# A new issue order for an attention and two-expert-layer kernel, from a planner with other prices, and a statistics buffer of eight turns

## The chip, the cores and the metric

The kernel runs on one core of a Trainium2 chip. The metric is device time in microseconds (us), lower is better; a value is the median of several runs. One further execution was recorded by the profiler; all rows below are from it. The engines are named as in the rows: PE (TensorE; PEld is its weight load), DVE (VectorE), ACT (ScalarE), POOL (GpSimd), and SP, which issues nearly all DMAs.

## The reference

```python
# q_l, k_l, v_l: (4, 8, 512, 64); q_g, k_g, v_g: (4, 8, 32, 64)
s_g = scale * q_g @ concat(k_g, k_l).T ;  out_g = softmax(s_g) @ concat(v_g, v_l)
s_l = concat(scale * q_l @ k_g.T, where(|i - j| <= 32, scale * q_l @ k_l.T, -1e9))
out_l = softmax(s_l) @ concat(v_g, v_l)
x = concat(out_g, out_l)                       # 2176 tokens x 512
h = x @ w_in ; solu = h * softmax(h)           # 512 -> 1024
x = layernorm(solu) * g_ln @ w_out             # 1024 -> 512
logits = x @ phi                               # 32 slots, 4 for each of 8 experts
slot_input = softmax(logits, axis=0).T @ x
slot_out[e] = relu(slot_input[e] @ w1[e]) @ w2[e]
out = softmax(logits, axis=1) @ slot_out       # 2176 x 512
```

## The kernel before

**Stages.** 16 local attention tiles (`local_tile`: 4 batches, 4 tiles of 128 queries) and 4 global ones (`global_tile`) give x. 17 dense tiles of 128 tokens (`dense_tile`) make h, its statistics, the normalised rows, the 32 logits, and add their part to the slot inputs as soon as x is there; attention, dense tiles and the loading of weights are interleaved over the first 230 us. `tail` runs the eight experts and the output product.

**What sets the order.** No order is written by hand. Every piece of work is an `op` with an engine, a price in ns and a number from the table `PRIORITY`. `Schedule.run` plays a time line with those prices: a free engine takes, among its ops whose inputs are ready in that time line, the one of lowest priority number. The result is one fixed sequence for each engine, and that sequence is what the program holds. On the chip each engine walks its own sequence and waits at a row whose inputs are late, whatever stands behind it. So a price, a cap or a priority acts only through the sequence; nothing of it is there at run time. The prices the change touches are:

- `LAT`: from the end of an op on one engine to the start of one on another; the entry `("DVE", "SP")` is that from a DVE copy to a DMA issue that reads it.
- `Fetch`: the planner holds that PE's instructions come in blocks of 256, and that a block can't be entered sooner than `TIME` ns after the one ahead of it was.
- `CAPS` and `KEEP`: how many buffers of a class may be alive at once, and how many are held back for a class. `STAY`: what PE adds to the priority of an op that changes its tiling.

**Lines the prediction speaks of.** L742: scores, one op is 32 products, which the profile counts as 64 matmuls. L755 (ACT): exp. L772: transposes of a tile of E, 4 to an op. L787, L862: attention times v. L899: x times `w_in`, half an op is 6 matmuls (wh, wl are high and low parts of the weights). L606, L607, L608 (DVE): three passes that make a weight, `W` or `wo`, out of the loaded words `wst`; L683 transposes `wo`. L983, L1049: logits and slot sums. L914 to L973 use the statistics `st`. L882: matmuls on a constant, into a bank that nothing reads (`warm`). In the tail L1177 and L1224 are the experts' products, L1258 the output product, L1264 and L1266 its copies by ACT and DVE, L1271 and L1273 the stores.

The last of the output, 192 columns wide, is stored in four DMAs of 384 KB and one small one:

```python
fs -> so -> sb                  # expert sums, once for 320 columns, once for 192
for j0 in range(0, 17, group):  # L1258, copies, then store() of one unit
    op("SP", ..., lambda store=store: store(nc.sync), obr, ())
```

Of the kernel before, what the change touches and what calls it, by code (L numbers as in the profile page):

```python
# [10 lines left out]
F32 = mybir.dt.float32  # L11
# [24 lines left out]
    ("SP", "SP"): 2600, ("PE", "SP"): 1270, ("ACT", "SP"): 1270, ("DVE", "SP"): 1270, ("Pool", "SP"): 1270,  # L36
# [68 lines left out]
class Fetch:  # L105
# [11 lines left out]
    def run(self, o, t, d):  # L117
        room = self.BLOCK - self.n % self.BLOCK
        if o.count >= room:
            self.entered = t + d * room / o.count  # L120
            self.TIME = 6400.0 if self.entered < 62000 else 5000.0
            self.n += o.count
            return True
        self.n += o.count
        return False


class Schedule:
# [8 lines left out]
    def buf(self, pool, tag, shape, dtype=F32, bufs=1):  # L137
        return Buf(self, pool, tag, shape, dtype, bufs, None)
# [228 lines left out]
def rank(names, name):  # L367
# [6 lines left out]
CAPS = dict(h=10, p1=67, E=20, W=52, eT=32, lT=8, ln=35, q=40, u=20, v=53, wst=20, xhl=72, xp=20)  # L374
KEEP = dict(p1=1, E=2, W=2, eT=2, eg=16, lT=1, ln=3, mkx=8, q=1, u=2, v=2, w=6, wo=5, wst=5, xhl=4, xp=1)
# [13 lines left out]
STAY = 1.13106627204  # L389
# [120 lines left out]
def kernel_body(ctx: ExitStack, tc: tile.TileContext, q, k, v, w_in, w_out, phi, gl, w1, w2, cst, out):  # L510
# [3 lines left out]
    buf, slot, op = sch.buf, sch.slot, sch.op  # L514
# [9 lines left out]
    mkx = slot("sb", "mkx", [128, 2, 512])  # L524
# [17 lines left out]
    wo = [Region(wob[f // 2], lambda a, f=f: a[:, f % 2, :]) for f in range(8)]  # L542
    egs = slot("sb", "eg", [128, 1024])
    eg = Region(egs, lambda a: a[:, 0:768])
# [341 lines left out]
    def dense_tile(j):  # L886
        X = xt[j]
        xhl = slot("sb", "xhl", [128, 2, 4, 128], F32R)
# [13 lines left out]
        st = buf("hw", "st", [128, 12], F32, 3)  # L902
# [532 lines left out]
```

## Time and profile before

| what | value |
|---|---|
| median of 3 runs | 295.19 us (294.35 to 296.47) |
| profiled execution | 295.09 us, of which 293.3 us are the span that the rows cover |
| PE busy | 265.0 us, 90% of the span, 4378 matmuls |
| DVE, ACT, POOL busy | 202.6 us, 196.1 us, 102.1 us |
| first matmul, end of the last one | 12.0 us, 286.1 us |
| PE clock | 1.00 of full speed in every stretch up to 285 us |
| DMA | 75.23 MB; mean 256 GB/s over the span |
| instruction packets of PE's queue (q8) | 34, 0.56 MB |
| kernel's share of the chain that ended last | PE 80%, DVE 6%, DMA 5%, ACT 4% |

Times in rows are from the span's start. A row of an instruction group has its start, its duration, engine, line, operation, the buffers written and read, and in brackets what its engine waited for just before. "issue" as a releaser means that the profile shows no instruction or transfer that the engine waited for. Matmuls overlap, so the duration of one is longer than the time it adds; in the chain of waits a piece has the time that it adds.

### The profile page before, as it was taken

The page shows a single profiled execution, that of the slowest core. Times are in us where ns is not written, and L with a number is a line of the kernel's source. Part 1 is how long each engine was busy: PE and PEld are TensorE (multiplying, and loading weights), DVE is VectorE, ACT ScalarE, POOL GpSimd, SP SyncE. Part 2 cuts the span into 40 slices and gives each one's busy share as a digit, 9 for nine tenths or more (in the row PEclk, how much of TensorE's full clock was granted, in tenths as well). Part 3 has the DMA queues.
Part 4 walks back from the last instruction along what each step waited for, and adds up shares of the span by engine and source line. Part 5 has one row for each costly group of instructions (what it writes and reads, how often), then busy time and mean ns, then how long its engine had stood idle before and what let it go on. Part 6 is the DMA issues. An engine that isn't in the chain of part 4 may idle for free.

```text
span 293.3 us, 10933 instructions
## 1 busy us (share of the span) xinstructions
PE 265.0 (90%) x4378; PEld 199.0 (68%) x4378; DVE 202.6 (69%) x752; ACT 196.1 (67%) x650; POOL 102.1 (35%) x171
## 2 busy tenths in 40 slices
PE   0259789999999999999999999989999999999990
PEld 0248577877877887787877878868778774354670
DVE  1889989999864799859797888379769840110450
ACT  3498998875897799997799876555567732020350
POOL 3787775922202516331321424134234333100000
PEclk9999999999999999999999999999999999999996
DMA  7999999916885002625892759986847997999476
GB/s 253 378 401 415 401 405 404 373 64 254 288 329 175 11 6 74 220 81 161 276 378 72 253 158 327 378 323 235 233 166 251 339 353 250 323 348 291 150 263 202
DMA packets 33532, 75.23 MB, mean 256 GB/s; under 512 B 2889, under 2 KB 15817, under 8 KB 33097
## 3 DMA queue, kind: packets, MB, share of 16 engines
q1 hardware_dynamic: 33348, 74.43, 72.0%
q8 instruction: 34, 0.56, 0.8%
q14 instruction: 18, 0.14, 0.1%
q10 hardware_dynamic: 132, 0.10, 0.1%
HBM read 67.83 MB, written 4.46 MB: 246 GB/s over the span
## 4 chain that ended last, share of the span: by engine, by line
PE 80%; DVE 6%; DMA 5%; ACT 4%; issue 2%; SPq 0%; DVEq 0%; ACTq 0%
PE h L899 30%; PE p L1224 5%; PE p L787 5%; PE p L742 5%; PE p L1177 5%; PE p L772 4%; PE p L962 4%; DMA q<-in_q 3%; PE p L983 3%; PE p L1049 3%; PE p L882 2%; PE p L862 2%; PE p L1258 2%; PE p L851 2%; DMA mkx<-in_cst 2%
## 5 line engine op out<-in xcount | busy, mean ns | idle before, releaser
L899 PE MATMUL h<-w,xhl 128*128 128x512 f32 x408 | 107.2, 405 | 0.9 <-issue 0.8
L899 PEld LDWEIGHTS h<-w,xhl 128*128 128x128 f32 x408 | 72.5, 188 | 17.7 <-issue 3.6
L755 ACT ACTIVATE E<-E,nmx 128x128 f32<-128x128 f32 x128 | 49.8, 394 | 1.9 <-DVE nmx L750 1.9
L742 PE MATMUL p<-k,q 64*32 64x128 f32 x1024 | 21.2, 291 | 16.8 <-DMA k<-in_k 12.0
L750 DVE CUSTOM_DVE_ANT_0 E<-p,mkx 128x128 f32<-128x128 f32 x128 | 28.9, 284 | 4.0 <-PE p L742 3.9
L742 PEld LDWEIGHTS p<-k,q 64*32 64x32 f32 x1024 | 15.9, 112 | 21.0 <-issue 15.8
L919 ACT ACTIVATE u<-h,st 128x512 f32<-128x512 f32 x34 | 23.1, 687 | 6.6 <-DVE st L915 6.6
L891 POOL TENSOR_TENSOR xhl<-xp,xhl 128x512 fp32r<-128x512 f32 x16 | 20.6, 1288 | 16.8 <-ACT xhl L890 16.6
L922 DVE SCALAR_TENSOR_TENSOR u<-h,u 128x512 f32<-128x512 f32 x34 | 22.9, 683 | 3.7 <-ACT u L919 3.5
L755 ACT ACTIVATION_READ_ACCUMULATOR E<-E,nmx 128x1 f32 x128 | 24.7, 193 | 0.0
L914 DVE TENSOR_REDUCE st<-h 128x1 f32<-128x512 f32 x34 | 22.5, 684 | 1.8 <-PE h L899 1.6
L772 PE MATMUL p<-cs,E 128*128 128x128 f32 x128 | 20.1, 288 | 1.2 <-ACT E L755 1.2
L774 ACT ACTIVATE eT<-p 128x512 f32<-128x512 f32 x32 | 18.4, 593 | 3.7 <-PE p L772 3.6
L968 ACT ACTIVATE u<-ln 128x1024 f32<-128x1024 f32 x17 | 18.1, 1062 | 3.4 <-DVE ln L941 3.4
L973 POOL TENSOR_TENSOR st<-st,eps 128x1 f32<-128x1 f32 x17 | 10.8, 635 | 25.9 <-DVE st L970 25.7
L787 PE MATMUL p<-v,eT 128*32 128x64 f32 x1024 | 18.8, 226 | 0.4 <-issue 0.2
L787 PEld LDWEIGHTS p<-v,eT 128*32 128x32 f32 x1024 | 16.6, 114 | 3.6 <-issue 1.2
L772 PEld LDWEIGHTS p<-cs,E 128*128 128x128 f32 x128 | 15.7, 149 | 4.3 <-ACT E L755 1.4
L967 ACT ACTIVATE lT<-p 128x512 f32<-128x512 f32 x25 | 14.3, 592 | 6.1 <-PE p L962 6.1
L926 POOL TENSOR_SCALAR st<-st 128x1 f32<-128x1 f32 x17 | 5.2, 307 | 34.2 <-ACT u L919 26.7
L794 DVE TENSOR_TENSOR eT<-p,r 128x256 f32<-128x256 f32 x32 | 12.6, 417 | 5.1 <-PE p L787 2.1
L617 POOL TENSOR_SCALAR W<-W 128x512 f32<-128x512 f32 x8 | 11.9, 1492 | 8.5 <-ACT W L616 8.5
(144 smaller groups left out, 550.6 us busy)
## 6 DMA issues: line engine op xcount, KB each, us to landing
unit<-in_w SPq DMA_DIRECT2D x47, 512.0 KB, 5.9
v<-in_v SPq DMA_DIRECT2D x28, 512.0 KB, 7.0
k<-in_k SPq DMA_DIRECT2D x3, 1536.0 KB, 6.4
k<-in_w SPq DMA_DIRECT2D x9, 512.0 KB, 5.1
wst<-in_w_in SPq DMA_DIRECT2D x8, 512.0 KB, 9.8
wst<-in_w_out SPq DMA_DIRECT2D x8, 512.0 KB, 9.1
q<-in_q SPq DMA_DIRECT2D x6, 512.0 KB, 5.6
out<-unit SPq DMA_DIRECT2D x8, 320.0 KB, 4.3
```

The lines of the kernel that those rows point to most:

```text
L742: nc.tensor.matmul(out=sp[hh][32 * c : 32 * c + 32, a2 + i, :], lhsT=Q[rows, 4 * (a2 + i) + c, :], rhs=K[rows, c, s : s + 128], start=True ...
L750: nc.vector.tensor_tensor_reduce(out=E[:, hh, a, :], in0=sp[hh][:, a, :], in1=MK(mask_kind(4 * t + a)), scale=-SCALE, scalar=3.0e38, op0=A ...
L755: nc.scalar.activation(out=E[:, hh, a, :], in_=E[:, hh, a, :], func=AF.Exp, bias=nmx[:, hh, a : a + 1], scale=-1.0, accum_out=sm[:, hh, a ...
L772: nc.tensor.transpose(out=tp[:, a, :], in_=E[:, hh, a, :], identity=I())
L774: op("ACT", 478, lambda hh=hh, tp=tp: nc.scalar.activation(out=eT[hh].ap, in_=tp.ap, func=AF.Copy), (tp,), (eT[hh],))
L787: nc.tensor.matmul(out=av[32 * c : 32 * c + 32, hh, a, :], lhsT=eT[hh][:, a, 32 * c : 32 * c + 32], rhs=V[:, (g - 1) % 2, 64 * h : 64 * h ...
L891: op("Pool", 1250, lambda: nc.gpsimd.tensor_tensor(out=xl.ap, in0=X.ap, in1=xh.ap.bitcast(F32), op=ALU.subtract), (X, xh), (xl,), port=True)
L899: nc.tensor.matmul(out=hp[n].ap, lhsT=lhs[:, kt, :], rhs=rhs[kt][n].ap, start=(kt == 0 and lhs is xh and rhs is whi), stop=(kt == 3 and lh ...
L914: op("DVE", 602, lambda n=n: nc.vector.tensor_reduce(out=part(7 + n), in_=hp[n].ap, axis=AX.X, op=ALU.max, negate=True), (hp[n],), (col[7 ...
L919: op("ACT", 664, lambda n=n: nc.scalar.activation(out=u[:, n, :], in_=hp[n].ap, func=AF.Exp, bias=nm(), scale=1.0, accum_out=part(7 + n)), ...
L922: op("DVE", 613, lambda n=n: nc.vector.scalar_tensor_tensor(out=u[:, n, :], in0=hp[n].ap, scalar=1.0, in1=u[:, n, :], op0=ALU.mult, op1=AL ...
L968: op("ACT", 1040, lambda: nc.scalar.activation(out=flat(), in_=ln.ap, func=AF.Square, accum_out=ssq()), (*cens, lT[0]) if last else (cen,) ...
```

## The change

The planner gets other prices and limits: 2000 ns instead of 1270 from ACT or DVE to an SP issue that reads their result; 8200 ns instead of 6400 for a block of instructions entered between 30 and 37 us of its time line; 60 ns more for an op of the output product; other caps, holds and tiling bias. The table `PRIORITY` is another one throughout. The ring of statistics buffers `st`, one of which a dense tile uses, has 8 turns instead of 3. With that, the sequences of all engines are made anew. No op is added or removed: both programs have the same count of every line on PE, and the same DMAs. One line is inserted above line 505, so lines behind it are one higher in the changed kernel (L742 is L743 there).

```diff
-    ("SP", "SP"): 2600, ("PE", "SP"): 1270, ("ACT", "SP"): 1270, ("DVE", "SP"): 1270, ("Pool", "SP"): 1270,
+    ("SP", "SP"): 2600, ("PE", "SP"): 1270, ("ACT", "SP"): 2000, ("DVE", "SP"): 2000, ("Pool", "SP"): 1270,
...
-            self.TIME = 6400.0 if self.entered < 62000 else 5000.0
+            self.TIME = 5000.0 if self.entered >= 62000 else 8200.0 if 30000 < self.entered < 37000 else 6400.0
...
-CAPS = dict(h=10, p1=67, E=20, W=52, eT=32, lT=8, ln=35, q=40, u=20, v=53, wst=20, xhl=72, xp=20)
-KEEP = dict(p1=1, E=2, W=2, eT=2, eg=16, lT=1, ln=3, mkx=8, q=1, u=2, v=2, w=6, wo=5, wst=5, xhl=4, xp=1)
+CAPS = dict(h=12, p1=63, E=23, W=58, eT=24, lT=9, ln=29, q=37, u=20, v=50, wst=18, xhl=73, xp=24)
+KEEP = dict(E=2, W=1, eT=2, eg=4, lT=1, ln=3, mkx=2, q=2, u=2, v=6, w=14, wo=13, wst=4, xhl=4, xp=1)
...
-STAY = 1.13106627204
+STAY = 1.25705078264
...
 PRIORITY = """
-    -183421268 -188124029 6107468 -191252955 -193517899 29194840 37980178 36241030 -25836497 -188321516 28516688 94766979 -40409399 32268522 76499126
...
-        st = buf("hw", "st", [128, 12], F32, 3)
+        st = buf("hw", "st", [128, 12], F32, 8)
...
-                    op("PE", max(0.417 * w + 20, 110) * 2 * m, cmm, (ct, sb), pos, tiled=2, count=4 * m)
+                    op("PE", max(0.417 * w + 20, 110) * 2 * m + 60, cmm, (ct, sb), pos, tiled=2, count=4 * m)
```

In the rows of a sequence below, names carry a running number of the buffer, which differs between the two programs.

**First place: PE behind the score op in which it halted at 35.8 us.** PE before, from the end of that score op (p_91 and p_92 are its banks) to the next one:

```order
L742 MATMUL p_92_560<-k_429,q_334 32x128
L899 MATMUL h_82_519<-w_527,xhl_390 128x512 x3
L899 MATMUL h_82_519<-w_336,xhl_390 128x512 x3
L899 MATMUL h_618<-w_161,xhl_536 128x512 x3
L899 MATMUL h_618<-w_147,xhl_536 128x512 x3
L772 MATMUL p_103_638<-cs_72,E_478 128x128 x4
L742 MATMUL p_106_650<-k_429,q_334 32x128
```

PE in the changed program, from the end of the score op at the same place (p_90 and p_91):

```order
L743 MATMUL p_91_558<-k_393,q_463 32x128
L900 MATMUL h_85_530<-w_515,xhl_391 128x512 x3
L900 MATMUL h_85_530<-w_335,xhl_391 128x512 x3
L900 MATMUL h_616<-w_454,xhl_539 128x512 x3
L900 MATMUL h_616<-w_147,xhl_539 128x512 x3
L900 MATMUL h_649<-w_161,xhl_539 128x512 x3
L900 MATMUL h_649<-w_103,xhl_539 128x512 x3
L684 MATMUL p_111_669<-cs_78,wo_603 128x128 x2
L743 MATMUL p_113_673<-k_393,q_463 32x128
```

What moved: a third half of a dense tile stands ahead, the transposes of E went behind, and the transposes of `wo_603` (before: `wo_605`, three halves of L899 later) came forward.

DVE in the changed program at that place, where `wo_603` is made (its sequence before has the same rows under other names, from E_561 to wo_605):

```order
L915 TENSOR_REDUCE st_627<-h_85_530 128x1
L751 ISA E_559,nmx_607<-p_90_557,mkx_81 128x128
L751 ISA nmx_607 128x1
L607 TENSOR_SCALAR p_102_637<-wo_603 128x512
L608 SCALAR_TENSOR_TENSOR p_102_637<-wst_474,p_102_637 128x512
L609 SCALAR_TENSOR_TENSOR wo_603<-wst_474,p_102_637 128x512
```

Nothing moved here: DVE still makes this weight behind the scores of the same tile and behind the first row maximum of h.

**Second place: PE around the 18th border of 256 instructions, near 130 us.** Before, from the dense tile that follows a score op:

```order
L899 MATMUL h_2378<-w_527,xhl_2030 128x512 x3
L899 MATMUL h_2378<-w_336,xhl_2030 128x512 x3
L1014 MATMUL p_366_2348<-cs_72,lps_2292 128x128
L1014 MATMUL p_371_2366<-cs_72,lps_2334 128x128
L851 MATMUL p_391_2472<-cs_72,eg_66 128x128 x3
L772 MATMUL p_394_2480<-cs_72,E_2034 128x128 x4
L983 MATMUL p_396_2489<-lT_2352,pb_1495 32x128 x8
L1049 MATMUL p_398_2501<-ln_2148,D_2478 32x256 x4
L1049 MATMUL p_399_2508<-ln_2104,D_2476 32x256 x4
```

The changed program, from the attention product of a global tile:

```order
L863 MATMUL p_350_2230<-v_968,eT_2420 32x64 x8
L984 MATMUL p_395_2496<-lT_2381,pb_1535 32x128 x8
L1050 MATMUL p_398_2508<-ln_2002,D_2489 32x256 x4
L788 MATMUL p_370_2362<-v_1408,eT_2159 32x64 x4
L788 MATMUL p_370_2362<-v_1391,eT_2159 32x64 x8
L788 MATMUL p_370_2362<-v_2122,eT_2159 32x64 x4
L1050 MATMUL p_400_2534<-ln_1379,D_2492 32x256 x4
L743 MATMUL p_402_2542<-k_2267,q_2261 32x128
L743 MATMUL p_403_2543<-k_2267,q_2261 32x128
```

What moved: no dense tile and no full transposes stand between these 256 instructions any more; they are 48 matmuls of L863, 16 of L984, 16 of L1050, 32 of L788 and the beginning of a score op.

**Third place: the end.** SP, the last stores before (unit_4826 is the second half of a pair whose first is unit_4821; unit_4843 comes from the output product after it):

```order
L1273 DMA out<-unit_4793 4x32x320
L1271 DMA out<-unit_4796 128x4x192
L1271 DMA out<-unit_4821 128x4x192
L1271 DMA out<-unit_4843 128x4x192
L1271 DMA out<-unit_4826 128x4x192
```

SP in the changed program (unit_4825 is the second half of that pair, unit_4848 comes after it):

```order
L1274 DMA out<-unit_4792 4x32x320
L1272 DMA out<-unit_4796 128x4x192
L1272 DMA out<-unit_4821 128x4x192
L1272 DMA out<-unit_4825 128x4x192
L1272 DMA out<-unit_4848 128x4x192
```

The last two stores changed places. PE at the last output product, before (between the banks p_823, p_824 and p_827, p_828 of the output product):

```order
L1258 MATMUL p_823_4811<-ct_4772,ct_4516 128x192
L1258 MATMUL p_824_4812<-ct_4772,ct_4516 128x192
L882 MATMUL p_688_4149<-cs_72 128x128
L1258 MATMUL p_827_4829<-ct_4772,ct_4516 128x192
L1258 MATMUL p_828_4830<-ct_4772,ct_4516 128x192
```

PE in the changed program at the same place:

```order
L1259 MATMUL p_823_4810<-ct_4771,ct_4513 128x192
L1259 MATMUL p_824_4811<-ct_4771,ct_4513 128x192
L883 MATMUL p_687_4147<-cs_78 128x128 x6
L1259 MATMUL p_827_4834<-ct_4771,ct_4513 128x192
L1259 MATMUL p_828_4835<-ct_4771,ct_4513 128x192
```

Five matmuls on a constant moved from behind the last output product to ahead of it.

## Rows read from the trace of the kernel before

**Rows 1.** Waits of PE: us in total, times, longest.
```profile
PE p L742 <- DMA k<-in_k: 12.0, 1, 12.0
...
PE p L742 <- issue: 2.2, 3, 1.7
PE p L683 <- DVE wo L608: 1.3, 1, 1.3
```

**Rows 2.** Busy time by stretch: start:end, length, five engines, clock, DMA share, GB/s.
```profile
36.00:244.00 208.00, 204.24 (x3401) 161.67 (x3400) 165.58 (x630) 159.96 (x543) 74.46 (x140) 1.00 0.67 236
```

**Rows 3.** Chain of waits, 35 to 41 us: start, us, what.
```profile
35.79 1.69 issue
37.47 0.45 PE p L742 x15
37.92 2.96 PE h L899 x12
```

**Rows 4.** DMA queues, 34 to 37 us: packets, MB, share of 16 engines.
```profile
q8 instruction: 1, 0.02, 2.1%
```

**Rows 5.** Stretches around two halts; the second count is that of weight loads.
```profile
0.00:171.55 171.55, 151.89 (x3006) 120.66 (x3010) 142.22 (x564) 142.97 (x496) 75.29 (x111) 1.00 0.68 246
0.00:174.10 174.10, 154.44 (x3136) 122.95 (x3136) 144.62 (x570) 144.59 (x499) 75.86 (x112) 1.00 0.67 243
...
0.00:186.34 186.34, 166.49 (x3258) 132.32 (x3262) 152.83 (x595) 152.34 (x522) 80.17 (x119) 1.00 0.69 248
...
0.00:190.85 190.85, 171.00 (x3388) 136.10 (x3389) 154.69 (x602) 153.92 (x526) 80.71 (x120) 1.00 0.70 251
```

**Rows 6.** As rows 2: ahead of these two halts, and near 130 us.
```profile
130.00:136.00 6.00, 6.00 (x182) 4.64 (x170) 5.78 (x31) 6.00 (x27) 1.36 (x4) 1.00 0.29 94
...
171.55:173.90 2.35, 2.35 (x136) 2.18 (x136) 2.19 (x7) 1.62 (x5) 0.57 (x1) 1.00 0.20 33
186.34:190.81 4.47, 4.47 (x145) 3.74 (x135) 1.82 (x7) 1.58 (x5) 0.50 (x1) 1.00 0.97 373
```

**Rows 7.** Timeline of PE, the first matmuls after these two halts.
```profile
174.37 0.42 PE L787 MATMUL p<-v,eT 128*32 128x64 f32 x14 [0.19 <-issue]
...
192.21 0.51 PE L899 MATMUL h<-w,xhl 128*128 128x512 f32 x1 [0.78 <-issue]
```

**Rows 8.** Chain of waits, 132 to 137 us: what four kinds of op add.
```profile
132.95 0.57 PE p L983 x16
133.53 0.92 PE p L1049 x16
134.45 0.80 PE p L862 x48
135.25 1.03 PE p L787 x64
```

**Rows 9.** Timeline of DVE, the end of the first `wo` weight after the halt.
```profile
42.05 0.69 DVE L608 SCALAR_TENSOR_TENSOR wo<-wst,p 128x512 int32<-128x512 int32 x1
```

**Rows 10.** Page, costliest groups: busy, mean ns, idle before it and its releaser.
```profile
L914 DVE TENSOR_REDUCE st<-h 128x1 f32<-128x512 f32 x34 | 22.5, 684 | 1.8 <-PE h L899 1.6
```

**Rows 11.** Timeline from 283 us: copies and warm matmuls, then SP's last two stores.
```profile
283.24 1.02 DVE L1266 COPY unit<-p 128x384 f32<-128x384 f32 x2 [0.43 <-PE p L1258]
...
284.58 0.56 DVE L1266 COPY unit<-p 128x384 f32<-128x384 f32 x1 [0.32 <-PE p L1258]
...
284.65 1.42 PE L882 MATMUL p<-cs 128*128 128x128 f32 x11
...
285.20 0.80 SPq L1271 DMA_DIRECT2D out<-unit  x1
...
286.05 1.49 SPq L1271 DMA_DIRECT2D out<-unit  x1
```

**Rows 12.** Stretch in which the last stores move; below it their time to landing.
```profile
285.00:291.00 6.00, 1.07 (x10) 0.83 (x8) 0.14 (x1) 0.24 (x2) 0.00 (x0) 0.74 0.92 283
...
DMA to landing us min/median/max: 6.1/6.2/6.3
```

204 rows, old and new, of the table PRIORITY are left out of this document.

## Prediction

> **What bounds the kernel now.** I read the waits of PE first, since PE is busy for 90% of the span. They are short [rows 1]: one wait of 12.0 us for the first keys, then nothing longer than 1.7 us. The busy time by stretch says how much is left: between 36 and 244 us PE works 204.24 of 208.0 us at full clock [rows 2]. DVE and ACT work 162 and 160 us there, so PE is the bound, and an order that lost no time at all would gain 208.0 − 204.24 = 3.8 us in that stretch, 1.3% of the whole. A new order can take away idle time of PE and nothing else, because both programs hold the same operations: the same count of each line on PE, and by the sequences 99 and 100 changes of PE's tiling.
>
> Before 36 us the sequences of all engines are the same up to a few swapped rows. The first scores still need the same loads, and the chain there goes through the same DVE rows. I take 0 for that stretch. From 219 us to the last output products the sequences again agree, and I take 0 there too.
>
> So three things are left: the halts of PE that are called "issue", new waits between 36 and 219 us, and the stores at the end.
>
> **The halts.** The waits put 2.2 us in three halts on L742 [rows 1]; the largest is 1.69 us at 35.79 us, inside a score op of which 15 matmuls are left [rows 3]. Its operands are there, since the products ahead of it read the same k and q. What is under way is an instruction packet of PE's queue [rows 4]. Two more halts are 0.19 and 0.78 us [rows 7]. Counting matmuls and weight loads between halts gives their rule: from 171.55 to 174.10 us it is 130 + 126 = 256, from 186.34 to 190.85 us 130 + 127 = 257 [rows 5]. PE goes on at 174.37 and 192.21 us [rows 7], that is 2.8 and 5.9 us after it crossed the border 256 instructions earlier; ahead of the first of these DMA moved 33 GB/s, ahead of the second 373 [rows 6]. I read it as a block of 256 instructions that comes some time after the one ahead of it was entered, later when DMA is busy. A halt is that time less the work that 256 instructions hold.
>
> The planner's 8200 ns is meant for the halt at 35.79 us. It lets the planner know of the wait; it doesn't make the packet come. In the changed program the border falls into the score op at the same place (first place in the sequences), and the operations of the block ahead of it are the same. I take a halt of the same size: **0**. The bounds are −1.7 (no halt) and +0.5.
>
> Elsewhere the work in a block changes. The densest new one is the 18th, near 130 us (second place in the sequences): 48 matmuls of L862, 16 of L983, 16 of L1049, half of 64 of L787 and about 15 of L742. That is 0.80 + 0.57 + 0.92 + 0.52 [rows 8] + 0.45 [rows 3] = 3.3 us. DMA moves 94 GB/s there [rows 6], so 2.8 us is the nearer price and there is no halt; by the dearer price, 5.9 us, it would be 2.6. Other blocks get longer or shorter by less than 1 us: the one before 88 us and the one before 191 us, which halt now, hold about 0.4 us more work each, and three that don't halt hold 0.2 to 0.7 less. I take **0** for all of these, with −1.5 (the halts of [rows 7] and half a us more go) to +1.7 (two thirds of the dear price in one block).
>
> The Trainium skill, page "Runtime: NRT & Kernel Launch", section "Instruction fetch mechanics", says that a sequencer fetches blocks of 256 instructions through a DMA queue of its own while the one ahead executes, and that crossing a border is mostly hidden. The count of 256 agrees with the two stretches of [rows 5]; that it is hidden does not, by the 1.69 us of [rows 3]. By that rule there would be no price for a border, and the sum below would be lower by 2.2 + 0.2 + 0.8 = 3.2 us [rows 1, 7].
>
> **A new wait at 42 us.** Behind the halt, PE before does twelve matmuls of L899 in 2.96 us, 0.247 each [rows 3]. In the changed sequence 18 matmuls of L899 stand there, from 37.92 us to 37.92 + 18 x 0.247 = 42.37, and behind them the transposes of a `wo` weight. DVE's rows ahead of that weight are the same as before, and its last pass ends at 42.05 + 0.69 = 42.74 us [rows 9]. The row maximum that DVE takes ahead of it reads the first six of these matmuls, as before, so DVE is not later. PE waits 0.37 us and the hand-over, together about **+0.6**. The bounds are 0 (halt longer by 0.5) and +1.3, what the same wait cost once before [rows 1]. Behind it in PE's sequence are the next scores; DVE still has work for 0.3 us and more, so nothing else runs dry.
>
> **The ring of eight.** L914, the first writer of `st`, waits for PE's h alone, 1.6 of its 1.8 us [rows 10], never for a buffer. More turns remove no wait and add no instruction: **0**, both ways.
>
> **The end.** The last DVE copies before end at 283.24 + 1.02 = 284.26 us, which makes the second store of the pair ready. SP doesn't issue it: the store ahead in its sequence waits for the copy that ends at 284.58 + 0.56 = 285.14, goes out at 285.20, and the ready one only at 286.05 [rows 11]. It lands 6.3 us later, at 292.3 [rows 12]. Swapped, the ready one goes out at about 284.3. The last one still needs the last output product, and in front of this stand five more warm-ups, 5 x (1.42/11) = 0.65 us at most [rows 11], about 0.5 since PE had a short idle there. It goes out at 285.14 + 0.5 = 285.7 instead of 286.05, 0.35 earlier. The DMA engines have 8% of 6 us = 0.5 us to spare between 285 and 291 us [rows 12], and the earlier store lets them use it and the time ahead of 285. So the gain is between 0.35 and 0.9; I take **−0.6**. The bounds are 0 (the warm-ups eat it all) and −1.7 (the ready store was issued 286.05 − 284.3 = 1.75 us late and all of it comes back).
>
> **The sum.** 295.09 (the profiled execution) + 0 + 0 + 0.6 + 0 − 0.6 = **295.1 us**. The profiled execution is 0.1 us under the median of the three runs, 295.19, so nothing has to be added for that.
>
> **Rivals.**
>
> *Halts go away.* The planner's price may make the sequence put other work where the halt was, or the fetch may be earlier for a reason that I don't see. The halt at 35.79 us and half of the others vanish, and the wait at 42 us grows into its bound, since PE is earlier by 1.7 us: 295.1 − 1.7 − 0.8 + 0.7 − (the rest of the tail) 0.4 = 292.9 us. For it speaks that all of PE's idle time between 36 and 244 us is 3.8 us [rows 2] and mostly of this kind; against it, that the same rows stand around the border. With the wait hidden too it is 292.2, the floor.
>
> *Dense blocks halt (the other side).* If the time to the next block is 5.9 us and not 2.8 in a stretch of light DMA, the 18th block halts for 2.6 us; the 20th, near 147 us, holds about 3.1 us of work and halts for 2.8 (before, it held little more and did not halt). Both: 295.1 + 5.4 = 300.5; one of them and some tenths in two others: 295.1 + 3.2 = 298.3 us, which is what I take for this rival. It decides when the packet lands more than about 1.5 us later than in the stretch at 171.55 us. Against it: DMA moves 94 GB/s there, and the cheap halt fell at 33, the dear one at 373 [rows 6].
>
> *Expert weights late.* A weight that lands later in the tail would hold the experts' products. The loads are the same and the tail's sequences too, so that it takes a buffer that comes free late; one wait would be 1 to 3 us, 297 us.
>
> *Nothing moves at all.* Wait and stores both come out at 0: 295.1 us, the same time as the forecast.
>
> **How the numbers follow.** One per cent, 2.95 us, is about what a measurement of this kernel can tell from no change. The forecast, with the case in which nothing moves, has 0.72; halts going away 0.13; dense blocks 0.10; late weights 0.05. The forecast's own range is 293.9 to 296.5: the wait's bounds and the tail's, 1.2 below, and 0.7 and 0.6 above with a tenth for the runs' spread. From the rivals the range takes the upper half of the first (to 292.6) and the lower half of the second (to 297.8): 292.6 to 297.8. Faster by over 1% means below 292.2: the first rival with nothing lost at 42 us, or a tail at its bound; 0.12. Slower by over 1%, above 298.1: the second rival or a long late weight; 0.12. The rest, 0.76, is within 1%.
>
> **What the changed profile would show.** Right: PE's waits again have "issue" on the scores with one of 1.5 to 2.2 us near 36 us; a new wait of L684's transposes for L609 of DVE, 0.4 to 0.8 us, near 42.5 us; PE busy 203.5 to 204.5 us between 36 and 244 us; no halt over 0.5 us near 130 us; SP's second-to-last store at 284 to 285 us, and the last one half a us or less behind 285.2. Wrong: no "issue" over 0.5 us near 36 us (the first rival), or one of over 1.5 us between 125 and 150 us (the second); a wait for a DMA in L1178 or L1225 (the third). The forecast would fail outright if PE lost more than 3 us in the stretch in which the sequences agree, before 36 us: there I did not work out each row.

## The result and the profile after

The changed kernel takes 299.01 us, the median of five runs (298.16 to 299.48). The kernel before, run beside it, takes 296.26 us (294.35 to 296.6). The ratio is 1.011, with a 95% interval of 1.007 to 1.015: it is slower by about 1%, some 3 us. The profiled execution took 299.48 us, 4.4 more than that of before (295.09); a stretch of 11 us holds as much as these 4.4.

PE is still the bound. Between 36 and 244 us it is busy for 202.66 of 208.0 us, against 204.24 before [rows 2], and the mean granted clock of the stretch is 0.99 instead of 1.00. Busy time by stretch of the changed kernel, columns as in rows 2:

```profile
36.00:244.00 208.00, 202.66 (x3354) 160.75 (x3355) 162.81 (x628) 160.59 (x543) 72.22 (x139) 0.99 0.66 229
...
49.00:50.00 1.00, 1.00 (x7) 0.86 (x5) 0.88 (x2) 0.14 (x2) 0.91 (x2) 0.95 1.05 388
50.00:51.00 1.00, 1.00 (x4) 0.61 (x4) 0.93 (x3) 0.00 (x0) 0.00 (x0) 0.50 1.02 398
51.00:52.00 1.00, 1.00 (x8) 0.67 (x6) 1.00 (x2) 0.00 (x0) 0.00 (x0) 0.50 0.97 382
52.00:53.00 1.00, 1.00 (x34) 0.83 (x33) 0.19 (x1) 0.60 (x1) 0.00 (x0) 0.50 0.53 201
53.00:54.00 1.00, 1.00 (x12) 1.00 (x9) 0.87 (x4) 0.18 (x1) 0.00 (x0) 0.84 0.15 61
```

From about 50 to 53 us PE runs at half clock (0.50, which is 1.2 GHz). What stands ahead of that is in its waits, which answer to [rows 1]:

```profile
PE p L743 <- issue: 2.6, 3, 1.6
...
PE p L788 <- issue: 2.2, 1, 2.2
PE p L684 <- DVE wo L609: 1.9, 2, 1.3
```

The 1.6 us on L743 is the halt of [rows 3], nearly unchanged. New are 2.2 us on L788 and, inside the last row, a second wait for a `wo` weight. The timeline of PE shows both in their place:

```profile
42.66 0.41 PE L684 MATMUL p<-cs,wo 128*128 128x128 f32 x2 [0.61 <-DVE wo L609]
43.00 1.16 PE L743 MATMUL p<-k,q 64*32 64x128 f32 x64
44.08 1.66 PE L900 MATMUL h<-w,xhl 128*128 128x512 f32 x6
45.58 0.38 PE L684 MATMUL p<-cs,wo 128*128 128x128 f32 x2
45.98 0.53 PE L788 MATMUL p<-v,eT 128*32 128x64 f32 x20
48.66 0.42 PE L788 MATMUL p<-v,eT 128*32 128x64 f32 x12 [2.16 <-issue]
49.01 2.19 PE L900 MATMUL h<-w,xhl 128*128 128x512 f32 x6
50.99 1.06 PE L773 MATMUL p<-cs,E 128*128 128x128 f32 x4
51.98 1.08 PE L788 MATMUL p<-v,eT 128*32 128x64 f32 x32
52.99 0.79 PE L773 MATMUL p<-cs,E 128*128 128x128 f32 x4
...
53.84 0.60 PE L773 MATMUL p<-cs,E 128*128 128x128 f32 x4
...
54.41 1.63 PE L900 MATMUL h<-w,xhl 128*128 128x512 f32 x6
```

PE idles 0.61 us at 42 us, works 3.8 us, halts for 2.16 us in the middle of 32 matmuls, and then runs slowly: six matmuls of L900 take 2.19 us where the same six take 1.63 at 54.41. The slow rows cost 0.56 on these six, 0.46 on the next four of L773 (1.06 against 0.60), 0.43 on the 32 of L788 (1.08 against 0.65 for the same 32 in the kernel before, at 51.88 us) and 0.19 on the last four: 1.6 us. So 0.6 + 2.2 + 1.6 = **4.4 us** between 42 and 53 us, as much as the whole difference. Elsewhere gains and losses cancel. The halts that before had near 174 and 192 us [rows 7] are gone, and two of 0.45 and 0.51 us stand at 94 and 166 us: between 54 and 244 us PE idles 1.3 us instead of 2.3. The end takes 0.5 us more (below). I did not follow each of the other small pieces.

Executions differ in their clock: the mean granted clock over the span is 0.980 to 0.989 in the five executions of the changed kernel, and of the 70 executions of the kernel before that ran beside the experiments, 24 are under 0.99 (median 296.1 us) and 46 are not (294.9 us).

That the halt sits at a border is in the counts: the stretches from the start to within either halt, when nothing runs.

```profile
0.00:36.50 36.50, 19.13 (x474) 15.03 (x474) 27.78 (x100) 26.42 (x83) 25.27 (x26) 1.00 0.98 373
0.00:48.00 48.00, 27.74 (x600) 21.32 (x601) 37.48 (x141) 37.23 (x126) 33.32 (x33) 1.00 0.99 380
```

Between them lie 126 matmuls and 127 weight loads; with the instructions that only wait, it is one block of 256. So it is with each wait of PE for "issue" in either trace: counting these three kinds of instruction, those of the changed kernel stand behind 962, 1217, 2753 and 5825, those of the kernel before behind 961, 2754, 5826, 6338 and 6850, whole blocks of 256 apart to within one.

PE's instruction packet for the border at 46.5 us starts at 46.09 us; none starts from 37 us to there. The DMA queues from 46.0 to 46.1 us show it (a packet counts where it starts; its share of 16 engines in 0.1 us is 1.03 us):

```profile
q8 instruction: 1, 0.02, 64.4%
```

It has landed at 47.12 us, and PE goes on 1.54 us later. At the nine halts just counted PE goes on 1.2 to 1.6 us after its packet has landed. In the kernel before the packet for the same border is under way from 42.9 to 43.9 us, and PE gets to the border only at 47.0. There is no halt there.

The end of the program, timeline and time to landing of the last store, against [rows 11, 12]:

```profile
287.35 0.88 PE L883 MATMUL p<-cs 128*128 128x128 f32 x6
...
288.91 0.56 DVE L1267 COPY unit<-p 128x384 f32<-128x384 f32 x1 [0.85 <-PE p L1259]
...
289.85 1.20 SPq L1272 DMA_DIRECT2D out<-unit  x1
...
DMA to landing us min/median/max: 6.8/6.8/6.8
```

The last copy ends at 289.47 us; the last store goes out at 289.85 and lands 6.8 us later, at 296.67, 7.2 us after the copy. Before it was 285.14 and 292.34, 7.2 us too. So the new order of the stores gives nothing here, and the last copy starts later by 0.5 us more than the copies of the pair ahead (4.33 and 3.80 us later than before), with the five warm-ups in front of its product. The end adds about 0.5 us.

### The profile page after: what moved, and what is told of

It is laid out like the page before. It is cut to its first block, busy times and chain, and to the rows that moved or that the text cites. A ratio compares the mean times of both kernels' runs of the same rounds, so it can differ in the third digit from the quotient of the medians.

```text
span 297.7 us, 10934 instructions
## 1 busy us (share of the span) xinstructions
PE 267.4 (90%) x4378; PEld 200.8 (67%) x4378; DVE 200.8 (67%) x752; ACT 197.2 (66%) x650; POOL 100.8 (34%) x171
## 4 chain that ended last, share of the span: by engine, by line
PE 86%; DMA 5%; DVE 3%; issue 2%; ACT 1%; SPq 0%; ACTq 0%
PE h L900 31%; PE p L743 6%; PE p L788 6%; PE p L773 5%; PE p L1225 5%; PE p L1178 5%; PE p L963 4%; PE p L984 3%; DMA q<-in_q 3%; PE p L1050 3%; PE p L863 2%; PE p L883 2%; PE p L1259 2%; DMA cs<-in_cst 2%; PE p L852 2%
## 5 line engine op out<-in xcount | busy, mean ns | idle before, releaser
L900 PE MATMUL h<-w,xhl 128*128 128x512 f32 x408 | 106.6, 405 | 0.1
L900 PEld LDWEIGHTS h<-w,xhl 128*128 128x128 f32 x408 | 73.1, 189 | 16.6 <-issue 1.2
L743 PE MATMUL p<-k,q 64*32 64x128 f32 x1024 | 21.4, 292 | 17.2 <-DMA k<-in_k 12.0
L915 DVE TENSOR_REDUCE st<-h 128x1 f32<-128x512 f32 x34 | 23.4, 688 | 11.4 <-PE h L900 11.1
L743 PEld LDWEIGHTS p<-k,q 64*32 64x32 f32 x1024 | 16.0, 112 | 20.8 <-issue 17.0
L974 POOL TENSOR_TENSOR st<-st,eps 128x1 f32<-128x1 f32 x17 | 9.6, 565 | 37.8 <-DVE st L971 37.8
L788 PEld LDWEIGHTS p<-v,eT 128*32 128x32 f32 x1024 | 17.5, 116 | 7.2 <-issue 4.0
L788 PE MATMUL p<-v,eT 128*32 128x64 f32 x1024 | 20.3, 229 | 2.2 <-issue 2.2
L773 PE MATMUL p<-cs,E 128*128 128x128 f32 x128 | 20.4, 299 | 0.7 <-ACT w L630 0.7
L773 PEld LDWEIGHTS p<-cs,E 128*128 128x128 f32 x128 | 16.6, 156 | 3.4 <-issue 1.4
L963 PE MATMUL p<-cs,ln 128*128 128x128 f32 x104 | 15.4, 278 | 0.0
```

Source lines behind the costliest of these rows:

```text
L743: nc.tensor.matmul(out=sp[hh][32 * c : 32 * c + 32, a2 + i, :], lhsT=Q[rows, 4 * (a2 + i) + c, :], rhs=K[rows, c, s : s + 128], start=True ...
L773: nc.tensor.transpose(out=tp[:, a, :], in_=E[:, hh, a, :], identity=I())
L788: nc.tensor.matmul(out=av[32 * c : 32 * c + 32, hh, a, :], lhsT=eT[hh][:, a, 32 * c : 32 * c + 32], rhs=V[:, (g - 1) % 2, 64 * h : 64 * h ...
L900: nc.tensor.matmul(out=hp[n].ap, lhsT=lhs[:, kt, :], rhs=rhs[kt][n].ap, start=(kt == 0 and lhs is xh and rhs is whi), stop=(kt == 3 and lh ...
L915: op("DVE", 602, lambda n=n: nc.vector.tensor_reduce(out=part(7 + n), in_=hp[n].ap, axis=AX.X, op=ALU.max, negate=True), (hp[n],), (col[7 ...
L963: nc.tensor.transpose(out=tp[:, n, :], in_=ln[:, f // 2, 128 * (f % 2) : 128 * (f % 2) + 128], identity=I())
```

## Experiments

Kernels are named by what they start from. Ratios are against the kernel before, run beside them.

**Fewer bytes queued ahead of the packets.** In the loop that emits the operations:

```diff
         o.fn()
+        if o.eng == "SP" and not o.ins:
+            loads += 1
+            if 24 <= loads < 48:
...                                 # small: a 4-byte tile of its own for each
+                nc.sync.dma_start(out=small, in_=cst[0:1, 0:1])
```

> The changed kernel, with a DMA of 4 bytes into a cell that nothing reads behind each of 24 loads (those that SP issues from about 23 to 45 us); sequences are otherwise the same. Since only some eight DMAs are under way at a time, about half as many bytes are queued. Theory A (the halts of PE at 36 and at 46.5 us in the changed kernel come from an instruction packet that stands in the DMA engines behind queued data; the halt at 46.5 also lets PE's clock fall): the packet of 45.5 us starts 3 us or more earlier, the halt of 2.2 us and the slow clock after it are gone, the one at 36 is under 1 us, and the time is 3 to 5 us under that of the changed kernel, 294 to 296 us. Theory B (a packet takes its time whatever is queued, or the halt has another cause): both halts stay within 0.4 us, the time within 0.7 us of 299.

> The kernel before with the same 24 DMAs of 4 bytes. Theory A: its halt of 1.7 us at 35.8 us shrinks by 1 us or more, everything else is as before: 293.5 to 295 us, 1 to 2 us under before. Theory B: the same as before within 0.5 us.

Changed kernel: 296.57 us, ratio 1.005 (1.001 to 1.008); before: 295.56, ratio 1.001 (0.999 to 1.004). The thinning worked (loads issued near 36 us land after 5 us instead of 8), but the packet hardly moved: it starts at 45.4 us in the one, 0.7 us earlier, and at 42.9 in the other, as without it. So theory A, which asked for 3 us or more, is wrong on its main point: the depth of the data queue is not what holds the packet. Theory B fails for the changed kernel too. It still became faster, by 1.8 us by the ratios and 2.4 by the medians, since PE got to the border 0.3 us later, the packet came 0.7 us earlier and PE went on 1.4 instead of 1.5 us after its landing; so the halt was shorter, and in the profiled execution the clock stayed up:

```profile
47.85 0.42 PE L788 MATMUL p<-v,eT 128*32 128x64 f32 x12 [1.06 <-issue]
```

Before, thinned, shows the clock by itself. PE halts 1.88 us at 35.85 us there, longer than without thinning, and then runs slowly over twelve matmuls of L899 (4.6 us instead of 3.0):

```profile
38.00:40.00 2.00, 2.00 (x19) 1.48 (x6) 1.35 (x12) 1.91 (x6) 1.92 (x2) 0.65 0.95 326
40.00:42.00 2.00, 2.00 (x6) 1.60 (x5) 1.32 (x6) 1.54 (x8) 2.00 (x2) 0.50 0.84 303
```

**Other borders.** 32 matmuls on zeros at the start, which count as 64 matmuls and 64 loads, half a block:

```diff
...                              # fw: zeros, 128x16; fp: a bank of PSUM
+    for _ in range(32):
+        nc.tensor.matmul(out=fp[0:16, 0:16], lhsT=fw, rhs=fw, start=True, stop=True)
     for i in order:
```

> The changed kernel, with 32 small matmuls on zeros at its start, where PE waits for the first keys anyway. They shift every border of 256 PE instructions to another place in the program, by half a block if each counts as two matmuls. Theory A (the halts sit at borders): no halt in the scores at 36.8 and in L788 at 46.5 us; halts, if any, come near 32, 43 and 54 us, together under 2 us, and the clock stays up: 295 to 297 us. Theory B (the halts belong to these operations or their inputs): they stay where they are, 298 to 300 us.

> The kernel before with the 32 small matmuls at its start. Theory A: the halts move off the scores at 35.8 us and off the rows at 174.4 and 192.2 us; new ones come at the moved borders; the time changes by up to 2 us to either side. Theory B: the same halts at the same operations, the same time within 0.5 us.

300.41 us (median of three executions; ratio 1.017, 1.010 to 1.024) and 301.85 us (1.024, 1.017 to 1.030). The halts left their places and came at others: in the changed kernel none at 36.8 and none at 46.5 us, but

```profile
34.13 0.41 PE L743 MATMUL p<-k,q 64*32 64x128 f32 x3 [1.94 <-issue]
...
110.03 0.37 PE L788 MATMUL p<-v,eT 128*32 128x64 f32 x11 [1.24 <-issue]
...
154.99 0.41 PE L743 MATMUL p<-k,q 64*32 64x128 f32 x4 [0.96 <-issue]
...
167.74 0.87 PE L773 MATMUL p<-cs,E 128*128 128x128 f32 x6 [0.90 <-issue]
```

That halts belong to borders is shown; that shifting them would gain was wrong. In the filled kernel before, one halt of 3.56 us near 157 us is followed by six microseconds at half clock. The kernel before loses by moved borders; for the changed kernel the ratio of 1.017 isn't clear of its own 1.011.

**One exchange, one move in the changed kernel.** The first puts six matmuls of L900 ahead of the 32 of L788 in which PE halts; the second puts the transposes for which PE waits at 42 us behind the score op and the half of L900 after it:

```diff
     order, est = sch.run()
+    order.remove(190); order.insert(order.index(580) + 1, 190)   # after_swap
+    order.remove(546); order.insert(order.index(620) + 1, 546)   # after_wo
```

> The changed kernel, with one pair of operations of PE exchanged: six matmuls of L900 (1.5 us) come ahead of the first 32 matmuls of L788 in which PE halts at 46.5 us. Nothing else is moved. Theory C (the loss is the halt of 2.2 us at 46.5 us plus the slow clock behind it; the packet comes at 45.5 us whatever PE does, and PE halts for what it arrives too early): PE arrives at 48.0 instead of 46.5 us, the halt is 0.5 to 1 us, the clock stays at 1.00, the time falls by 2.5 to 3.5 us to about 296. Theory D (the packet is asked for by PE's own progress, so that it comes later when PE arrives later): the halt stays at about 2 us, the time within 0.7 us of 299.

> The changed kernel, with the transposes of the first wo weight, for which PE waits 0.61 us at 42.05 us, moved behind the score operation and the half of L900 that follow them. Theory C: the wait of 0.61 us goes, but PE is then 0.6 us earlier at the border, so that the halt at 46.5 us grows from 2.2 to 2.8 us; the time is the same within 0.5 us. Rival: the wait is worth its 0.6 us or more, and 298.2 us or less is measured.

The exchange: 298.33 us (1.011, 1.007 to 1.014), by the ratio no gain over the changed kernel, where theory C asked for 2.5 us or more; its profiled run took 297.81, 1.7 us less. The packet starts at 46.0 us, where it was, the halt fell to 1.07 us and the clock stayed up, as theory C says, but then PE waits for the next `wo` weight, which DVE hasn't made yet:

```profile
48.61 0.49 PE L788 MATMUL p<-v,eT 128*32 128x64 f32 x18 [1.07 <-issue]
...
51.67 0.44 PE L684 MATMUL p<-cs,wo 128*128 128x128 f32 x2 [0.81 <-DVE wo L609]
```

The move: **296.17 us** (1.003, 1.001 to 1.006). I had expected no gain, a wait that only turns into a longer halt. It gained 2.2 us by the ratios and 2.8 by the medians, because the packet came 1.7 us earlier with it (44.39 instead of 46.09 us), the halt all but went, and the clock stayed up:

```profile
42.84 1.14 PE L743 MATMUL p<-k,q 64*32 64x128 f32 x62 [0.21 <-DVE wo L609]
...
46.25 0.53 PE L788 MATMUL p<-v,eT 128*32 128x64 f32 x20 [0.26 <-DVE nmx L751]
47.03 0.42 PE L788 MATMUL p<-v,eT 128*32 128x64 f32 x12 [0.25 <-issue]
```

Of the 3 us that the change costs, this one row of PE's sequence holds more than two.

**A gap in the loads.**

```diff
+            if loads in (27, 28, 29, 30):   # one tile for all four, so each waits for the last
+                nc.sync.dma_start(out=small, in_=cst[0:1, 0:1])
```

> The changed kernel, in which SP pauses its loads once: behind four loads issued near 25 to 29 us it writes 4 bytes into the same cell, each after the one before has landed. So the data that are under way run out near 38 to 40 us, and DMA is only about half busy from there to 45 us; later loads come some 5 us later. Theory F (a packet of instructions can't get through while the DMA engines are saturated with data, however short the queue): the packet that came at 45.5 us starts by 41 us, within 1 us of a gap in the data, and PE does not halt at 46.5 us. Theory G (it is asked for late): it still starts at 44 us or later. The time itself says little, since loads are late: 295 to 303 us.

Two runs, 295.09 (the profiled one) and 299.92 us; too few for a time. The DMA engines were half idle at 37 to 38 and again at 41 to 42 us, and a quarter idle up to 44:

```profile
37.00:38.00 1.00, 0.81 (x16) 0.57 (x17) 0.27 (x3) 1.00 (x5) 0.82 (x1) 1.00 0.50 197
41.00:42.00 1.00, 0.94 (x5) 0.43 (x3) 0.96 (x2) 1.00 (x6) 1.00 (x2) 1.00 0.49 194
42.00:43.00 1.00, 0.43 (x10) 0.29 (x18) 1.00 (x2) 1.00 (x6) 1.00 (x1) 1.00 0.73 169
```

and the packet still starts at 45.2 us, as theory G says; theory F falls. That it was asked for late is not shown by this: the share is a mean over 16 engines, and the one that carries the packet may have been busy.

**The price alone, the ring alone.** The first edit is this one, the second the line of `st` in the change.

```diff
-            self.TIME = 6400.0 if self.entered < 62000 else 5000.0
+            self.TIME = 5000.0 if self.entered >= 62000 else 8200.0 if 30000 < self.entered < 37000 else 6400.0
```

> The kernel before with one number changed: 8200 ns instead of 6400 for the instruction block entered between 30 and 37 us; table, limits, ring and the other prices are those of before. The sequences are the same up to the score operation in which PE halts at 35.8 us; behind its twelve matmuls of L899 the planner now puts the transposes of the first wo weight, as in the changed kernel (there behind eighteen). Theory E (the price makes the planner believe in a longer halt than the chip has, so that it places work that isn't ready): the halt at 35.8 us stays at 1.2 to 1.9 us, PE waits for that weight 1.5 to 2 us near 41 to 43 us, and the time is 1 to 3 us over before: 296.3 to 298.3 us. Rival (the price is right and only the table lost): no such wait, 294.5 to 295.5 us.

> The kernel before with 8 turns of st instead of 3, nothing else; the planner's sequences of PE change from its 58th operation on (from about 65 us), those before stay. The ring as such costs and gains nothing (no wait for it in the profile of before); what is measured is a new sequence with the work between borders shared out anew: within 1.5 us of before to either side, with the halt at 35.8 us unchanged and no wait at 42 us. If the ring were what loses the time: 298 us or more.

352.04 us (ratio 1.194) and 311.57 us (1.058), far more than expected: with the old table and one new constant the planner makes other sequences, in which PE waits for DVE and ACT in many places from 60 us on. But up to 50 us the first of the two is readable, and repeats the changed kernel with the loads of the kernel before (their order is the same up to 42 us):

```profile
37.98 4.36 PE L899 MATMUL h<-w,xhl 128*128 128x512 f32 x18
42.97 0.41 PE L683 MATMUL p<-cs,wo 128*128 128x128 f32 x2 [0.63 <-DVE wo L608]
```

Eighteen matmuls instead of twelve, then the `wo` transposes with the same wait: this order comes from the 8200 ns. And its packet starts at 46.3 us, where the same loads with the old order had it at 42.9. So the late packet goes with PE's sequence, not with the order of the loads. In the second, the halt at 35.8 us is there (1.69 us) and no wait at 42. The ring without the planner's answer to it:

```diff
-            b.tile = pools[b.pool].tile(b.shape, b.dtype, name=f"{b.tag}_{seq[0]}", tag=b.tag, bufs=b.bufs)
+            b.tile = pools[b.pool].tile(b.shape, b.dtype, name=f"{b.tag}_{seq[0]}", tag=b.tag, bufs=8 if b.tag == "st" else b.bufs)
```

> The kernel before with 8 places for st in memory, while its planner still plans with 3: every engine's sequence is word for word that of before. So this is the ring alone. Theory: no instruction waited for a place in it, so the time is that of before within 0.4 us. Rival: the waits for a free place were hidden in others, and the time falls by 0.5 us or more.

295.22 us, ratio 0.999 (0.996 to 1.001): nothing.

**The end.**

```diff
+    order.remove(1553); order.insert(order.index(1561) + 1, 1553)   # before_stores
+    for x in (1535, 1534, 1533, 1532, 1408):                        # after_tail
+        order.remove(x); order.insert(order.index(1562) + 1, x)
```

> The kernel before, with only the last two stores of SP exchanged. If the stores in the changed kernel gained 0.55 us, as its profile says against the kernel before, this gains the same: 0.4 to 0.8 us under before, 294.7 us or so, the last landing at 291.5 to 291.9 instead of 292.3 us. Rival: the last store queues behind more data and lands as late; 0 to 0.2 us.

> The changed kernel, with five of the six warm-ups ahead of the last output product put back behind it; the new order of the last two stores is kept. By the profiles the five cost 0.54 us and the order of the stores gave that much back. So the last store goes out 0.5 us earlier after the last product but one, and the time falls by 0.3 to 0.6 us. Rival: the last transfers are bound by the DMA engines, and nothing is gained.

The exchanged stores in the kernel before: 295.1 us, ratio 0.999 (0.997 to 1.001); the last one lands 7.4 us after the last copy instead of 7.2. The warm-ups put back: 298.92 against 299.01 us, and the last store lands 7.6 us after the last copy, 9.5 us after the copies of the pair ahead began, where it was 9.6 with them in front. So neither gains, as the rivals say: when the store ahead goes out a us earlier, or the last copy ends half a us earlier, the last landing comes at most 0.1 us earlier. That the DMA engines bind it is the likely reason, which no run tests. The second run also repeats the trace of the changed kernel at 46 us, halt and half clock behind it:

```profile
48.78 0.42 PE L788 MATMUL p<-v,eT 128*32 128x64 f32 x12 [2.15 <-issue]
...
50.00:53.00 3.00, 3.00 (x40) 2.29 (x38) 2.25 (x4) 0.60 (x1) 0.12 (x1) 0.50 0.86 333
```

## Why the prediction was wrong

- *PE bounds, and only its idle time can move*: half right. Idle time moved (5.3 instead of 3.8 us of the 208), but PE's busy time moved too, by 2.4 us over the span, some 1.6 of them through the clock. The prediction took the clock as given, 1.00 in each stretch, and had no term for it.
- *The halt at 35.79 us stays*: right, 1.63 us against 1.69. The planner's 8200 ns doesn't make the packet come.
- *"Elsewhere the work in a block changes ... I take 0"*: this is the step that failed. I looked at the blocks that had become dense, near 88, 130, 147 and 191 us, and not at the block right behind the known halt, because it was not dense: some 9 us of PE's time, where my dearest price was 5.9. But PE went on at 48.66 us, 11.4 us after it had left the halt ahead. The term was mis-sized by 2.2 us, and by 3.8 with the clock behind it. Two prices from two halts were no bound for a third one, and the stretch with the busiest DMA was the one I took no price from.
- *The 18th block does not halt*: right (3.0 us from border to border, and no gap), so the rival of dense blocks had the right mechanism, a block that comes later than PE is done with the one ahead, at the wrong place. The Trainium skill, page "Runtime: NRT & Kernel Launch", section "Instruction fetch mechanics", says that crossing a border is mostly hidden. Most borders of this trace agree, but not all: with 34 packets, two borders cost 1.6 and 2.2 us and two more 0.5 us each.
- *A new wait at 42 us of 0.6 us*: right (0.61), and it is 0.60 to 0.63 in five other kernels with that order. But I took it as a term by itself, with "nothing else runs dry" behind it. With it in place the packet came at 46.1 us, without it at 44.4, and the kernel is more than 2 us faster.
- *The ring costs nothing*: right.
- *The end, −0.6*: wrong. In the profile the end adds 0.5 us, outside the bounds of −1.7 and 0; the two runs on it move the time by 0.1 to 0.2 us. The step that failed is that an earlier issue lands earlier: the exchanged store went out at 284.24 instead of 286.05 us, and the last landing stayed.

What stays open is what makes PE's packet late. It starts at 42.7 to 44.1 us in the kernels with the order of before at that place, 5.1 to 5.7 us behind the border ahead, and at 44.4 to 46.3 us in those where eighteen matmuls stand behind the halt, 6.8 to 8.9 us behind that border. Half the depth of the data queue or a gap in the loads moves it by less than 1 us, and it doesn't go with the loads' order. Asked for at a fixed instruction it is not either: in the thinned kernel before, at half clock, PE was some 60 instructions into the block when it started, and some 200 without that. That the clock fell because of the idle time ahead of it is what the order of events suggests, no more: it fell behind 0.61 + 2.16 us of idle time and behind 1.88 us, and stayed up behind 1.69 us and behind 0.61 + 1.06. But it also stayed up behind 1.91 us, in the kernel before with eight places for `st` (38 to 40 us, clock 1.00), so the length of a halt alone doesn't decide it.

## What to carry to other kernels

A model of the chip that plans the order may make a stall longer to be safe, but it then fills the stall with what it believes to be ready; here that was a wait of 0.6 us. Price a new wait with what follows it on the same engine (the next instruction border, the clock), not by its own length. And constants of a planner and a table tuned under them are one thing: each part alone is no test of the part (352 and 312 us here).

## What was not expected of the hardware

- Instruction packets of PE started from 0.1 us after a border (71.74 to 71.80 us in the changed kernel, no data moving) to 8.8 us after (37.27 to 46.09 us, DMA at over 400 GB/s), and thinning or pausing the loads shortened the longest of these times by no more than 1 us.
- Shifting the borders by half a block cost the kernel before 2.4%.
- After halts of 1.88, 2.03, 2.16 and 3.56 us PE's granted clock was 0.50 for 3 to 6 us, and each of these so cost nearly twice its own length; after halts of 1.91 and 1.94 us it was not.
